# Zero products in the state's PSUM bank, a strided read of the turned r, and new order tables, in an RWKV and MLP-mixer kernel

## The chip, the cores and the metric

The kernel runs on one core of one Trainium2 chip. A core has five engines with a queue each: TensorE (PE; its weight loads are shown as PEld), VectorE (DVE), ScalarE (ACT), GpSimd (POOL) and SyncE (SP), which here only starts transfers. 16 DMA engines move data between the chip's memory, the on-chip memory SBUF and, for transposes, within SBUF. TensorE writes to PSUM, eight banks of 512 fp32 columns on 128 partitions. The metric is the device time of one execution in microseconds (us), lower is better.

## The reference

Two steps, all in fp32 for the reference. First a linear attention with decay over 768 steps, for 4 batches and 8 heads of 48 columns; then a mixer on its result, `x`, with 768 tokens of 384 columns:

```python
for t in range(S):
    cur = np.einsum('bhd,bhe->bhde', u[None] * kt, vt)
    y[:, :, t] = np.einsum('bhd,bhde->bhe', rt, state + cur)
    state = w[None, :, :, None] * state + np.einsum('bhd,bhe->bhde', kt, vt)
...
h = np.maximum(xt @ w_tok1, 0.0) @ w_tok2
u = x + h.transpose(0, 2, 1)
h2 = np.maximum(u @ w_ch1, 0.0) @ w_ch2
return (u + h2).astype(np.float32)
```

`w_tok1` is 768 by 256, `w_tok2` 256 by 768, `w_ch1` 384 by 1536, `w_ch2` 1536 by 384; `xt` is `x` with tokens and columns exchanged.

## The kernel before

**Tiles.** The steps of a batch are cut into six units of 128, so there are 24 units. Heads lie in pairs, four pairs of two heads, each head padded from 48 to 64 columns. In a unit (`unit`, line 539) k is multiplied by powers of the decay (`kr<-kt,wn`), and r by the inverse powers, so that a unit's scores are plain products of k and r. Both are turned, so that head columns lie on partitions; `scores` (line 649) makes the products of turned k and turned r (`at_ps`, eight of 128 columns); two masked copies (`AT`) follow on DVE; `outputs` multiplies them with v (`vb`, v as bf16) and adds the state times r (`y_ps`); each step's own term is v times a sum over r, u and k (`adg`, then `yd` or `ydb`). The result goes to `x_b`. The state is collected in a PSUM tile `kv_ps` (`add_state`, line 666), over three units at a time, and copied to SBUF after each unit (`keep_state`, line 679).

**Batch 0 and the others.** In batch 0 r comes in windows of two units (`window`, line 513): `rwin` holds even and odd steps side by side, two products with powers (`wp2`) fill the two halves of `krw`, eight PE transposes make `tr_ps`, whose layout is (partition, odd or even, pair, step), and `evac_r` (line 530) brings even and odd steps together in `rkb`. k is turned by four transposes (`trk`) and copied to `rka`. Its own terms come from a product of turned k and r (`pr`) and four small matmuls (`ad_ps`), and are added by PE (`ydb` through the identity). Batch 1 turns k and r together on PE (`tr_ps`, `rk`); batches 2 and 3 turn them by DMA. `krw` and `kr` tiles have padding columns, set to zero once at the start (lines 371 to 373).

**Mixer** (`mixer`, line 744). Per batch: `h1_ps` (12 products of 384 columns, from `x_b` and `wtok1`), `h1r` (ReLU), then for batches 0 and 1 `hx_ps`, which gathers turned `x` and the product with `wtok2`, and `uT`, its copy; for batches 2 and 3 `hT_ps`, `u_sb` and a DMA transpose to `uT`. Then, for two halves of the batch, twelve `z_ps` (three products of 384 each, `wch1` times `uT`), their ReLU `zr`, and for each of three units twelve products `h_ps` (`zr` times `wch2`), `osb` and a store. The first `z_ps` of batch 0 is the first of 288.

**Order.** Nothing is scheduled while the program is built: every piece of work is recorded as a task (`Plan`, line 189), and `run` issues the tasks in the order of the table `ORDER` (line 21). Each engine executes its own part of that order strictly. `BUFS` (line 66) says which buffer of a pool each tile takes, `ENGINES` (line 159) which of two engines runs a task that may run on either (`flex`). `W_DEP` and `GATES` (lines 170, 171) tie weight transfers to loads and loads to weight transfers: a transfer with such an entry is not started before the named one has landed. Loads and stores are started by SP, in that order, too, weight transfers by POOL. A transfer is also not started before the one eight places earlier in the round of semaphores has landed.

All engine calls go through one helper, so that nearly every row of the profile has line 263; rows are told apart by their tiles. The profile leaves numbers at the end of names out: `h1_ps` and `h2_ps` are both `h_ps` there, `wtok1` and `wtok2` are `wtok`, `wch1` and `wch2` `wch`, `wp2` `wp`; `h1r`, `kr0` and `krw0` appear as `h1r`, `kr` and `krw`.

**Zero products.** `keep_warm` (line 926) multiplies a tile of zeros by a tile of zeros; nothing reads its result. `NWARM` (line 172) of them, 11, stand in `ORDER`, with 512 columns each and a PSUM buffer of the pool `m`, as other tasks have. The pool `m` has seven buffers, the state's `kv` one, eight banks together.

**The start.** ACT starts four small loads of w and u (`w_row`, `u_row`, `w_heads`, `u_heads`; lines 340 to 345), loads its function table (line 346), and computes powers of w as exponentials: `lnw`, then `wn`, `wp2` and `wp`, each 384 columns.

Of the kernel before, what the change touches and what calls it, by code (L numbers as in the profile page):

```python
# [67 lines left out]
    0, 1, 2, 0, 1, 2, 0, 1, 2, 0, 2, 0, 1, 2, 0, 1, 2, 1, 0, 1, 2, 0, 1, 0,  # L68
],
    'AT1': [  # L70
    0, 1, 2, 0, 1, 2, 0, 1, 2, 0, 2, 0, 1, 2, 0, 1, 0, 1, 2, 1, 0, 2, 1, 0,
# [11 lines left out]
    0, 1, 2, 3, 4, 0, 1, 2, 3, 0, 4, 1, 3, 4, 0, 2, 1, 3, 0, 4, 1, 3, 2, 0,  # L83
# [5 lines left out]
    0, 1, 2, 3, 1, 0, 3, 2, 1, 0, 3, 0, 0, 3, 2, 1, 0, 2, 3, 0, 2, 1, 2, 0,  # L89
# [5 lines left out]
    0, 1, 2, 3, 4, 5, 0, 2, 3, 1, 4, 5, 0, 2, 3, 1, 4, 0, 5, 2, 3, 1, 4, 0,  # L95
],
    'ku': [
    0, 1, 2, 0, 1, 0, 1, 2, 1, 0, 1, 2, 1, 0, 2, 2, 2, 2,
# [13 lines left out]
],  # L112
    'osb': [
    0, 1, 2, 2, 0, 2, 0, 2, 1, 2, 2, 0, 1, 0, 2, 1, 0, 2, 1, 0, 2, 1, 0, 2, 1,
# [5 lines left out]
    0, 1, 2, 3, 0, 2, 3, 1, 0, 2, 3, 0, 2, 1, 0, 3, 1, 0,  # L120
],
    'rka': [
    0, 1, 2, 1, 1, 0,
# [5 lines left out]
    0, 1, 0, 1, 0, 1, 0, 1, 0, 1, 0, 1, 0, 1, 0, 1, 0, 1,  # L129
],  # L130
    'rt': [
    0, 1, 2, 3, 4, 0, 2, 3, 1, 4, 0, 3, 4, 0, 3, 1, 4, 0,
],
    'rwin': [
    0, 1, 2,
],
    'uT': [
    0, 1, 2, 3, 0, 1, 3, 2,
],
    'u_sb': [  # L140
    0, 1, 2, 1,
],
    'vb': [
    0, 1, 2, 3, 4, 0, 1, 2, 3, 4, 0, 1, 2, 2, 4, 3, 0, 2, 0, 4, 1, 2, 4, 0,
],
    'vt': [
    0, 1, 2, 3, 4, 5, 0, 1, 2, 3, 4, 5, 0, 1, 2, 3, 4, 5, 0, 1, 2, 4, 3, 5,
],
    'yd': [
    0, 1, 2, 0, 1, 0, 1, 2, 0, 1, 0, 2, 1, 0, 2, 0, 1, 1,  # L150
],
    'ydb': [
    0, 1, 0, 1, 0, 1,
],
    'zr': [
    0, 1, 2, 0, 1, 0, 2, 0,
],
}
ENGINES = [
# [64 lines left out]
def kernel(  # L224
# [70 lines left out]
    def row(src):  # L295
        return src.rearrange("h d -> (h d)")
# [68 lines left out]
    def make_mask():  # L365
        pool.memset(mask, 1.0)
        pool.affine_select(out=mask, in_=mask, compare_op=ALU.is_gt, fill=0.0, base=0, pattern=[[1, 128]],
                           channel_multiplier=-1)

    t_mask = once("POOL", "mask", make_mask)  # L370
    t_kw0 = [once("DVE", "memset_m", lambda t=t: dve.memset(t, 0.0)) for t in krws]
    t_kp0 = [once("DVE", "memset_m", lambda t=t: dve.memset(t[:, 0], 0.0)) for t in krs]
    t_rp0 = [once("DVE", "memset_m", lambda t=t: dve.memset(t[:, 1], 0.0)) for t in krs]

# [588 lines left out]
```

## Time and profile before

| | us |
|---|---|
| median of 3 runs (169.28 to 170.26) | 170.03 |
| the profiled execution, its own time | 169.46 |
| its span, first to last instruction | 167.6 |
| PE busy (1449 matmuls) | 157.2 |
| DVE busy | 132.1 |
| POOL busy | 72.7 |
| ACT busy | 72.4 |

| group of rows | count | mean ns |
|---|---|---|
| PE `z_ps`, 384 columns | 288 | 327 |
| PE `h_ps` from `wch` and `zr`, 384 columns | 276 | 326 |
| DVE `AT` from `at_ps` and mask | 48 | 681 |
| DVE `rkb` from `tr_ps`, 1024 elements | 2 | 1280 |
| ACT `rkb` from `tr_ps`, 1024 elements | 1 | 1303 |
| DVE `rk` from `tr_ps`, 1024 elements | 2 | 692 |
| ACT `rk` from `tr_ps`, 1024 elements | 4 | 1013 |
| PE `idle_ps`, zero products of 512 columns | 11 | 537 |

The span is what the profiler saw, from the first to the last instruction; the execution's own time has some 1.9 us around it. A PE row's mean is the time one matmul takes from start to end; matmuls overlap, so the distance from one to the next is shorter (51 `z_ps` products follow each other in 8.29 us, 163 ns each), and the distance is what a sum needs. PEclk is the clock that TensorE was granted as a share of full speed. A DMA share is how busy the 16 DMA engines are on average; overlapping packets can bring it over 1.

### The profile page before, as it was taken

To read this page: it belongs to the slowest core of one execution; us is meant where nothing else is said; L and a number is where in the kernel's file an instruction comes from. 1 tells how busy PE (TensorE), PEld (TensorE's weight loads), DVE (VectorE), ACT (ScalarE), POOL (GpSimd) and SP (SyncE) were. 2 spreads that over 40 slices of the span, in tenths; PEclk is the share of its full clock that TensorE was granted. 3 is DMA by queue.
4 is the path that set the end of the run, shared out by engine and by line. 5 is a ranking of instruction groups with operands and counts; after the bars stand their busy time and mean duration, and the time that the engine had idled before them with its cause. 6 is when DMAs were issued, how large, how long until landed. Compare 5 with 4: busy or idle time off the path is not lost.

```text
span 167.6 us, 3756 instructions
## 1 busy us (share of the span) xinstructions
PE 157.2 (94%) x1449; PEld 105.9 (63%) x1449; DVE 132.1 (79%) x257; ACT 72.4 (43%) x158; POOL 72.7 (43%) x88
## 2 busy tenths in 40 slices
PE   6696999799999999999999999999999999999991
PEld 2273768566766777776656666667666666666671
DVE  7899978985898699999699999988988248446322
ACT  3991856467540475577934224156401201504100
POOL 4043956676344737459796789962100000000000
PEclk9999557999999999999999999999999999999999
DMA  5999998999999369899999999999510143501122
GB/s 112 243 250 193 214 183 162 176 188 209 221 209 215 75 152 234 190 201 203 160 209 219 227 204 213 158 254 234 125 47 0 51 101 111 117 0 53 47 94 94
DMA packets 94997, 26.59 MB, mean 159 GB/s; under 512 B 89730, under 2 KB 94084, under 8 KB 94980
## 3 DMA queue, kind: packets, MB, share of 16 engines
q1 hardware_dynamic: 92624, 23.11, 67.9%
q0 software_dynamic: 2160, 3.15, 11.5%
q8 instruction: 11, 0.18, 0.5%
q10 hardware_dynamic: 196, 0.11, 0.2%
q14 instruction: 6, 0.05, 0.1%
HBM read 20.46 MB, written 4.72 MB: 150 GB/s over the span
## 4 chain that ended last, share of the span: by engine, by line
PE 62%; DMA 13%; POOL 7%; DVE 7%; SPq 3%; issue 2%; ACT 2%; ACTq 1%; POOLq 0%
PE h_ps L263 24%; PE z_ps L263 21%; DMA rt<-in_r_dram 5%; PE y_ps L263 4%; PE at_ps L263 4%; SPq L263 3%; POOL rku L263 3%; DMA uT<-u_sb 3%; DMA kt<-in_k_dram 3%; PE tr_ps L263 2%; POOL kr L263 2%; DMA wp<-in_w_dram 2%; PE kv_ps L263 2%; DVE krw L263 2%; DVE rkb L263 1%
## 5 line engine op out<-in xcount | busy, mean ns | idle before, releaser
L263 PE MATMUL h_ps<-wch,zr 128*128 128x384 bf16 (+1 forms) x300 | 53.6, 320 | 0.0
L263 PE MATMUL z_ps<-uT,wch 128*128 128x384 bf16 x288 | 52.0, 327 | 0.7 <-DMA uT<-u_sb 0.4
L263 ACT ACTIVATE zr<-z_ps 128x384 bf16<-128x384 f32 x59 | 28.5, 491 | 35.2 <-PE z_ps L263 30.2
L263 PEld LDWEIGHTS <-wch 128*128 128x128 bf16 x288 | 31.6, 114 | 14.3 <-DMA uT<-u_sb 0.5
L263 PEld LDWEIGHTS <-zr 128*128 128x128 bf16 x300 | 27.4, 98 | 15.5
L263 DVE TENSOR_TENSOR AT<-at_ps,mask 128x512 bf16<-128x512 f32 x48 | 31.0, 681 | 1.6 <-PE at_ps L263 1.4
L263 DVE TENSOR_SCALAR zr<-z_ps 128x384 bf16<-128x384 f32 x37 | 19.8, 554 | 11.4 <-PE z_ps L263 11.3
L263 POOL TENSOR_TENSOR yd<-vb,adg 128x384 f32<-128x384 bf16 x13 | 11.9, 919 | 14.1 <-DVE adg L263 7.1
L263 POOL TENSOR_TENSOR kr<-kt,wn 128x384 bf16<-128x384 f32 x12 | 12.8, 1068 | 5.1 <-PE tr_ps L263 3.3
L263 PEld LDWEIGHTS <-kr 128*128 128x128 bf16 x152 | 11.3, 107 | 5.5 <-issue 3.8
L263 POOL TENSOR_TENSOR rku<-ku,rt 128x384 f32<-128x384 f32 x12 | 12.2, 1026 | 5.8 <-DMA rt<-in_r_dram 3.2
L263 ACT CAST vb<-vt 128x384 bf16<-128x384 f32 x18 | 9.2, 513 | 12.3 <-DMA vt<-in_v_dram 8.4
L263 DVE TENSOR_TENSOR osb<-u_sb,h_ps 128x384 f32<-128x384 bf16 (+1 forms) x13 | 6.8, 523 | 9.3 <-PE h_ps L263 9.1
L263 POOL TENSOR_TENSOR kr<-rt,wp 128x384 bf16<-128x384 f32 x10 | 10.3, 1033 | 5.0 <-DMA rt<-in_r_dram 4.9
L263 PEld LDWEIGHTS <-rk 48*128 48x128 bf16 (+1 forms) x204 | 7.9, 95 | 5.0 <-issue 2.8
L263 POOL TENSOR_TENSOR ku<-kt,u_bc 128x384 f32<-128x384 f32 x10 | 10.4, 1042 | 1.2 <-DMA kt<-in_k_dram 1.1
L263 ACT CAST S<-kv_ps 48x192 bf16<-48x192 f32 x26 | 8.1, 313 | 5.7 <-PE kv_ps L263 5.4
L263 DVE TENSOR_TENSOR x_b<-y_ps,yd 128x384 bf16<-128x384 f32 x18 | 9.8, 552 | 0.8 <-PE y_ps L263 0.7
L263 DVE TENSOR_REDUCE adg<-rku 128x8 f32<-128x384 f32 x18 | 9.7, 545 | 0.5 <-POOL rku L263 0.4
L263 DVE TENSOR_TENSOR kr<-kt,wn 128x384 bf16<-128x384 f32 x12 | 8.4, 703 | 1.7 <-DMA kt<-in_k_dram 1.7
L263 PE MATMUL y_ps<-vb,AT 128*128 128x48 bf16 x192 | 9.2, 188 | 0.0
L263 PEld LDWEIGHTS <-wtok 128*128 128x128 bf16 x72 | 6.8, 98 | 3.8
(96 smaller groups left out, 205.8 us busy)
## 6 DMA issues: line engine op xcount, KB each, us to landing
kt<-in_k_dram SPq DMA_DIRECT2D x24, 192.0 KB, 4.3
vt<-in_v_dram SPq DMA_DIRECT2D x24, 192.0 KB, 3.9
out_dram<-osb SPq DMA_DIRECT2D x23, 192.0 KB, 2.4
rt<-in_r_dram SPq DMA_DIRECT2D x18, 192.0 KB, 4.4
wch<-in_moe_w_ch_dram POOLq DMA_DIRECT2D x4, 384.0 KB, 6.6
rwin<-in_r_dram SPq DMA_DIRECT2D x3, 384.0 KB, 4.4
wtok<-in_moe_w_tok_dram POOLq DMA_DIRECT2D x2, 384.0 KB, 6.0
wch<-in_moe_w_ch_dram POOLq DMA_DIRECT2D x1, 768.0 KB, 9.6
```

The costliest lines, as they stand in the source:

```text
L263: return lambda *args, **kw: tc.keep_in_program_order(f(*args, **kw))
```

## The change

1. `NWARM` goes from 11 to 153. A zero product has 128 columns instead of 512 and takes no buffer of pool `m`: the state's tile is now a whole bank of 512 columns, of which the state has the first 384, and zero products write the last 128. The very first ones, before there is a state, take a bank of their own of the same buffer. All of them are placed in the first batch, up to the first `z_ps`.
2. `evac_r` copies the same elements in another order: it now reads `tr_ps` alternating between even and odd steps (1024 bytes apart) and writes `rkb` in one run; before, it read in runs and wrote every other element.
3. The zeroing of `kr` and `krw` can run on DVE or POOL, and `krw` is zeroed in halves. The function table's load stands behind the load of `w_row`.
4. `ORDER`, `BUFS`, `ENGINES`, `W_DEP` and `GATES` are new: other orders on all engines, other engines for a part of the tasks, one entry in `GATES` in place of four, and the zero products' places.

```diff
-W_DEP = [(0, 4, 1), (0, 3, 0), (1, 0, 0), (1, 0, 1), (1, 1, 2), (1, 1, 0), (1, 1, 1)]
-GATES = {(1, 5, 1): 5, (1, 5, 2): 1, (3, 0, 1): 4, (3, 3, 0): 1}
-NWARM = 11
+W_DEP = [(0, 1, 2), (0, 4, 2), (0, 3, 2), (0, 5, 2), (1, 0, 0), (1, 1, 1), (1, 4, 0)]
+GATES = {(1, 2, 2): 1}
+NWARM = 153
...
-    t_tab = once("ACT", "act_table", lambda: act.preload_act_table_set("natural_log_exp_and_others"))
+    t_tab = once("ACT", "act_table", lambda: act.preload_act_table_set("natural_log_exp_and_others"), [t_wrow])
...
-    t_kw0 = [once("DVE", "memset_m", lambda t=t: dve.memset(t, 0.0)) for t in krws]
-    t_kp0 = [once("DVE", "memset_m", lambda t=t: dve.memset(t[:, 0], 0.0)) for t in krs]
-    t_rp0 = [once("DVE", "memset_m", lambda t=t: dve.memset(t[:, 1], 0.0)) for t in krs]
-
+    ZERO = {"DVE": "memset_m", "POOL": "memset_mp"}
+
+    def zero(t):
+        return flex(ZERO, lambda on: engine_of[on].memset(t, 0.0))
+
+    t_kp0 = [zero(t[:, 0]) for t in krs]
+    t_rp0 = [zero(t[:, 1]) for t in krs]
+
+    t_kw0 = [zero(t[:, j]) for t in krws for j in range(2)]
...
-    kv = [None]
+    kv, bank = [None], [None]
+
+    def new_bank(tag):
+        bank[0] = psum.tile([128, 512], f32, name="kv_ps", tag=tag, bufs=1)
+
...
-            copy(on, W["ra"].rearrange("p a c t -> p a (c t)").rearrange("p a (s j) -> p j a s", j=2), W["tr"])
+            copy(on, W["ra"].rearrange("p a c t -> p a (c t)").rearrange("p a (s j) -> p a s j", j=2),
+                 W["tr"].rearrange("p j a s -> p a s j"))
...
-                kv[0] = ps("kv_ps", [128, HP, 2, D], of="kv")
+                new_bank(f"kv{plan.buf('kv')}")
+                kv[0] = bank[0][:, 0:dm].rearrange("p (a q d) -> p a q d", a=HP, q=2)
...
     def keep_warm():
-        z = ps("idle_ps", [128, 512])
-        pe.matmul(z, warm[:, 0:128], warm, start=True, stop=True)
+        fresh = bank[0] is None
+        if fresh:
+            new_bank("kv0")
+        pe.matmul(bank[0][:, dm:512], warm[:, 0:128], warm[:, 0:128], start=fresh, stop=True, skip_group_check=True)
 
     for _ in range(NWARM):
-        add("PE", "warm", keep_warm, [t_warm], take=("m",))
+        add("PE", "warm", keep_warm, [t_warm])
```

The kind names in quotes (`"memset_mp"`, `"copy1024w"`) only label tasks and reach no engine. What the tables do to the work around the first batch, as the built order has it: 37 zero products come before the first `at_ps` product, 116 between it and the first `z_ps`. Of the products that scale k and r in batch 0, six run on POOL in place of two, one after the other: half of r window 0, `kr2`, `kr3`, half of r window 1, `kr3` again, half of r window 2. On DVE no work of batch 1 stands ahead of batch 0's `h1r`; before, two products of k or r, one of k and u, and one cast of v did. Eight transposes, eight scores and four state products of batch 1 stood ahead of the first `z_ps` on PE and now follow it. ACT's load of `w_heads` waits for the first load of k to land.

More of the change, by code (lines that the diff above doesn't have):

```diff
@@ L67 @@
     'AT0': [
-    0, 1, 2, 0, 1, 2, 0, 1, 2, 0, 2, 0, 1, 2, 0, 1, 2, 1, 0, 1, 2, 0, 1, 0,
+    0, 1, 2, 0, 1, 2, 1, 2, 0, 2, 0, 1, 2, 0, 1, 2, 0, 1, 2, 1, 0, 2, 0, 1,
 ],
     'AT1': [
-    0, 1, 2, 0, 1, 2, 0, 1, 2, 0, 2, 0, 1, 2, 0, 1, 0, 1, 2, 1, 0, 2, 1, 0,
+    0, 1, 2, 0, 1, 2, 0, 2, 1, 2, 1, 0, 2, 1, 0, 2, 1, 0, 2, 0, 1, 2, 1, 0,
 ],
@@ L82 @@
     'adg': [
-    0, 1, 2, 3, 4, 0, 1, 2, 3, 0, 4, 1, 3, 4, 0, 2, 1, 3, 0, 4, 1, 3, 2, 0,
+    0, 1, 2, 3, 4, 1, 2, 0, 3, 1, 4, 0, 3, 2, 1, 4, 0, 3, 2, 1, 0, 3, 4, 2,
 ],
@@ L88 @@
     'kp': [
-    0, 1, 2, 3, 1, 0, 3, 2, 1, 0, 3, 0, 0, 3, 2, 1, 0, 2, 3, 0, 2, 1, 2, 0,
+    0, 1, 2, 3, 3, 0, 2, 1, 3, 0, 3, 3, 1, 2, 3, 0, 1, 1, 2, 1, 0, 3, 1, 3,
 ],
@@ L94 @@
     'kt': [
-    0, 1, 2, 3, 4, 5, 0, 2, 3, 1, 4, 5, 0, 2, 3, 1, 4, 0, 5, 2, 3, 1, 4, 0,
+    0, 1, 2, 3, 4, 5, 0, 1, 2, 3, 4, 5, 0, 1, 2, 4, 3, 5, 0, 1, 2, 4, 3, 0,
 ],
     'ku': [
-    0, 1, 2, 0, 1, 0, 1, 2, 1, 0, 1, 2, 1, 0, 2, 2, 2, 2,
+    0, 1, 2, 1, 2, 1, 0, 2, 1, 0, 1, 0, 2, 1, 2, 2, 0, 0,
 ],
@@ L103 @@
     'm': [
[8 rows of a table removed]
[8 rows of a table added]
 ],
     'osb': [
-    0, 1, 2, 2, 0, 2, 0, 2, 1, 2, 2, 0, 1, 0, 2, 1, 0, 2, 1, 0, 2, 1, 0, 2, 1,
+    0, 1, 2, 0, 0, 2, 2, 1, 2, 0, 1, 0, 2, 0, 1, 2, 0, 1, 2, 0, 1, 2, 0, 1, 2,
 ],
@@ L119 @@
     'rk': [
-    0, 1, 2, 3, 0, 2, 3, 1, 0, 2, 3, 0, 2, 1, 0, 3, 1, 0,
+    0, 1, 2, 3, 1, 3, 0, 2, 1, 3, 0, 1, 3, 2, 1, 0, 2, 3,
 ],
     'rka': [
-    0, 1, 2, 1, 1, 0,
+    0, 1, 2, 2, 0, 1,
 ],
@@ L128 @@
     'rku': [
-    0, 1, 0, 1, 0, 1, 0, 1, 0, 1, 0, 1, 0, 1, 0, 1, 0, 1,
+    0, 1, 0, 1, 0, 1, 0, 1, 0, 1, 1, 0, 1, 0, 1, 0, 0, 1,
 ],
     'rt': [
-    0, 1, 2, 3, 4, 0, 2, 3, 1, 4, 0, 3, 4, 0, 3, 1, 4, 0,
+    0, 1, 2, 3, 4, 1, 0, 2, 4, 3, 0, 1, 4, 3, 1, 0, 4, 2,
 ],
@@ L137 @@
     'uT': [
-    0, 1, 2, 3, 0, 1, 3, 2,
+    0, 1, 2, 3, 1, 0, 3, 2,
 ],
     'u_sb': [
-    0, 1, 2, 1,
+    0, 1, 2, 0,
 ],
     'vb': [
-    0, 1, 2, 3, 4, 0, 1, 2, 3, 4, 0, 1, 2, 2, 4, 3, 0, 2, 0, 4, 1, 2, 4, 0,
+    0, 1, 2, 3, 4, 0, 1, 2, 3, 4, 0, 2, 1, 4, 3, 1, 2, 0, 2, 1, 4, 1, 0, 2,
 ],
     'vt': [
-    0, 1, 2, 3, 4, 5, 0, 1, 2, 3, 4, 5, 0, 1, 2, 3, 4, 5, 0, 1, 2, 4, 3, 5,
+    0, 1, 2, 3, 4, 5, 0, 1, 2, 3, 4, 5, 0, 1, 2, 3, 4, 5, 0, 1, 2, 3, 4, 5,
 ],
     'yd': [
-    0, 1, 2, 0, 1, 0, 1, 2, 0, 1, 0, 2, 1, 0, 2, 0, 1, 1,
+    0, 1, 2, 0, 1, 2, 1, 0, 2, 1, 1, 2, 0, 2, 1, 1, 0, 2,
 ],
     'ydb': [
-    0, 1, 0, 1, 0, 1,
+    0, 1, 0, 0, 1, 0,
 ],
     'zr': [
-    0, 1, 2, 0, 1, 0, 2, 0,
+    0, 1, 2, 0, 1, 0, 2, 1,
 ],
@@ L340 @@
     t_wrow = once("ACT", "dma_tiny", lambda: act.dma_start(w_row, row(w).unsqueeze(0)))
-    t_wh = once("ACT", "dma_tiny", lambda: act.dma_start(
+    t_wh = once("ACT", "dma_tiny2", lambda: act.dma_start(
         w_heads.rearrange("h (q d) -> h q d", q=2)[:, :, 0:D], w.unsqueeze(1).to_broadcast([H, 2, D])), [t_wh1])
-    t_urows = once("ACT", "dma_tiny", lambda: act.dma_start(
+    t_urows = once("ACT", "dma_tiny2", lambda: act.dma_start(
         u_heads.rearrange("h (q d) -> h q d", q=2)[:, :, 0:D], u.unsqueeze(1).to_broadcast([H, 2, D])), [t_uh0])
-    t_urow = once("ACT", "dma_tiny", lambda: act.dma_start(u_row, row(u).unsqueeze(0)))
-    t_tab = once("ACT", "act_table", lambda: act.preload_act_table_set("natural_log_exp_and_others"))
+    t_urow = once("ACT", "dma_tiny2", lambda: act.dma_start(u_row, row(u).unsqueeze(0)))
+    t_tab = once("ACT", "act_table", lambda: act.preload_act_table_set("natural_log_exp_and_others"), [t_wrow])
     t_ones = once("DVE", "memset_s", lambda: dve.memset(ones, 1.0))
@@ L536, in window @@
         t_tr = add("PE", "tr_all", turn_r, [m0, m1, t_id], take=("m",), use=[(m0, "krw")])
-        W["t"] = flex({"ACT": "copy1024", "DVE": "copy1024d"}, evac_r, [t_tr], take=("rkb",), use=[(t_tr, "m")])
+        W["t"] = flex({"ACT": "copy1024w", "DVE": "copy1024v"}, evac_r, [t_tr], take=("rkb",), use=[(t_tr, "m")])
     def unit(b, c):
```

129 rows, old and new, of tables (BUFS, ENGINES, ORDER) are left out of this document.

## The prediction

> **What bounds the kernel now.** I read the page's slices first, then the busy time of TensorE (PE) in stretches, then the chain of waits, then the instructions in order of time. The slices of the profiled execution (40 equal parts of 167.6 us, 4.19 us each):
>
> ```profile
> PE   6696999799999999999999999999999999999991
> DVE  7899978985898699999699999988988248446322
> POOL 4043956676344737459796789962100000000000
> PEclk9999557999999999999999999999999999999999
> DMA  5999998999999369899999999999510143501122
> ```
>
> From slice 9 on PE is full almost to the end, so time can be saved only before that, in the first batch. There slices 5 to 7 show a granted clock of half speed. The stretches between the points where the clock changes are 3.41 us long; columns are stretch, its length, PE busy (instructions), clock, DMA share, GB/s:
>
> ```profile
> 10.22:13.63 3.41, 3.13 (x22) 1.00 1.09 211
> 13.63:17.04 3.41, 2.11 (x26) 1.00 1.06 207
> 17.04:20.45 3.41, 3.04 (x50) 0.50 1.10 219
> 20.45:23.87 3.42, 3.12 (x41) 0.50 1.13 177
> 23.87:27.28 3.41, 3.41 (x48) 0.50 1.00 172
> 30.69:34.10 3.41, 2.22 (x28) 1.00 1.05 153
> ```
>
> After the stretch with 2.11 us busy the clock fell; the one with 2.22 us did not lose it. It came back after 3.13 and after 3.41 us, not after 3.04 or 3.12. So here the clock is held by about 2.2 us of work in 3.41, and won by about 3.13. The 1.00 before 13.63 us is no measurement: the chain has four transposes of 128 columns in 0.43 us there, and eight in 0.45 us later, so TensorE ran at half speed (107 ns a product) up to about 13.6 us and again from 17.0 to 27.3, and at full speed (56 ns) otherwise.
>
> ```profile
> 8.29 0.43 PE trk L263 x4
> ...
> 29.40 0.63 DVE kr L263
> 30.03 1.27 DVE ku L263
> 31.30 1.10 DVE vb L263
> 32.40 0.47 DVE kr L263
> ...
> 36.81 8.29 PE z_ps L263 x51
> ...
> 47.92 0.45 PE tr_ps L263 x8
> ```
>
> The chain also shows VectorE (DVE) spending 3.47 us on products and a cast of the second batch just before the first batch's last `h1r`. From the first `z` at 36.81 us PE runs on to 164.25 with 0.7 us of waits; the last store ends at 167.6. I call the first scores product that waits for `rkb` S (16.30 us), the first `z` Z (36.81 us); Z to the end is 130.8 us.
>
> **The change, part by part.** Counts are from the built order of the changed kernel, durations from rows of before.
>
> *Zero products.* 11 of 512 columns go, 153 of 128 columns come: 37 before S, 116 between S and Z, none later. At 56 ns the 116 cost 6.5 us of PE's queue, at 107 ns 12.4 us. They are in order, so each holds back what is behind it unless PE would have waited.
>
> *S.* Four of the first batch's early products (half of r windows 0 and 1, `kr2`, `kr3`) go from DVE to GpSimd (POOL): six POOL products in a row (0.96 us apart, rows of 1.00) from about 6.6 us, when the second power for r is done. DVE loses 1.2 us of memsets ahead of `kr0`, which then starts when its power is ready, near 5.1 instead of 5.99 us. POOL's six memsets of 512 columns are unseen: its row for 128 columns is 0.20 us, so 0.2 to 0.8 each; I take 0.5, 3 us in all, done by 5.9 and hidden ahead of the first product at 6.6 (at 0.8 they would add 1 us). ScalarE's `w_heads` load now waits for the first k load, and `lnw` stands behind it; k loads land 2.8 to 5.7 us after their issue, this one's is at 0.81, so 3.6 to 6.5, against `lnw` at 3.91; I take the early end, 0.1 us, since nothing is loading yet. On PE the first window's transposes stand behind `ud`, and that behind `kr1`, `rka` and a small product on DVE: about 9.6 us. Then, at half speed, eight transposes (0.87), `trk` (0.43), 15 zero products (1.61), `trk` (0.43; its k load is SP's sixth, lands near 10.4, and POOL takes 1.0) and 6 zero products (0.64): S = 13.6 us, 2.7 sooner; 12 if the clock is up, 15.6 if DVE is held up (below).
>
> *The turned r.* Three evictions read with a step and write in one run. Rows: 1.28 us (DVE) and 1.30 (ScalarE) with the stepped write; 0.69 and 1.01 for 1024 elements with no step. No row has a stepped read: from 0.69 to twice the stepped row, 2.6. I take 1.28, no change, the row that still has a step: the first then ends before 13 us and PE arrives later; the others lie beside PE's work. At 2.6 S would be 14.4 and the time 169.4. The Trainium skill ("SBUF — State Buffer", section "Door 1: The DMA port swizzle") speaks against this edit: lines of 16 bytes in SBUF and 8 in PSUM, and a penalty for each access that goes to a new line. The old write steps by 4 bytes and stays in a line four times; the new read steps by 1024 bytes and changes lines at each element, so by it the new eviction is the dearer one and 169.4 the sum. That the old step should then have cost nothing does not agree with 1.28 against 0.69 us.
>
> *S to Z.* PE's real work at full speed: 48 scores at 41 ns (2.0), outputs 48 at 25 and 20 at 42 ns (2.0), states 24 at 42 ns and one 384 (1.2), six `ydb` at 163 (1.0), 24 transposes and 18 `hx` at 56 (2.4), 24 `ad` at 25 (0.6), 24 of `h1` and `hx` at 163 (3.9): 13.1 us. With 6.5 us of zero products 19.6. DVE's list from `rkb` to `h1r` (twelve masks at 0.60, five `pr` at 0.33, seven others at 0.47, small ones) is 13.2 us, and from `h1r` to Z another 2.9: below PE's, since the 3.47 us of second-batch work are gone. So PE becomes the bound of this stage. Half speed after S: with PE fed, one stretch should win the clock; half a stretch on average is 1.7 us at half speed, 0.85 us lost (0 to 5.1). Three zero products wait for ScalarE's copy of the state from the same bank, with scores, `ad` and outputs behind them; the copy (0.65 a pair) ends near PE's arrival: 0.4 us (0 to 1.5). Z = 13.6 + 13.1 + 6.5 + 0.85 + 0.4 = 34.45, 2.36 us sooner.
>
> *After Z.* Of the second batch, 8 transposes, 8 scores and 4 state products, done ahead of Z before, now follow: 0.45 + 0.33 + 0.17 = 0.95 us. `wch1_1` (9.6 us to land) is triggered behind a POOL product that needs `ad`, and from that `ad` to the first use PE has 9.3 us of work: 0 to 1.5, I take 0, as other waits of PE will lie between. Loads must follow a Z that is 2.4 us sooner. They are full (share 1.05 to 1.16) from 4 to 118 us but for one hole, where a store waits at the head of SP's queue:
>
> ```profile
> 54.00:60.00 6.00, 6.00 (x81) 4.36 (x79) 4.00 (x8) 3.18 (x5) 3.82 (x4) 1.00 0.37 72
> 60.00:98.00 38.00, 37.70 (x419) 25.94 (x417) 36.32 (x68) 21.30 (x48) 25.48 (x26) 1.00 1.09 204
> ```
>
> A share of 0.37 over 6 us leaves 3.8 us; with Z sooner that store is ready sooner, so up to 3.8 us can be followed. The new load order and gates I price at -0.3 to 2 us, at 0. Products move from DVE (9.6 us less, of 132.1) to POOL (12 more, on 72.7): both stay below PE's 157.
>
> Sum: -2.36 + 0.95 = -1.4 us. Against the profiled execution: span 167.6 to 166.2, its time 169.46 to 168.1. That execution lay 0.6 us below the median of 170.03, so the median becomes 168.6.
>
> **Rivals.**
> *The clock stays down (slower).* The zero products sit in PE's queue; at 107 ns they cost 12.4 us. If PE runs 10.2 us at half speed after S, as it did before, Z = 13.6 + 19.6 + 5.1 + 0.4 = 38.7, +1.9, with 0.95 more: +2.85, 172.9 us. It decides from 4.5 us at half speed after S. For: stretches of 3.04 and 3.12 us busy did not win the clock, and waits for POOL's products leave such holes. Against: at half speed PE has the longest list, so it fills its own stretch.
> *POOL locks DVE out (no change).* Rows at 11.45 us:
>
> ```profile
> 11.45 2.41 DVE L263 TENSOR_TENSOR krw<-rwin,wp 128x384 bf16<-128x384 f32 x1
> 11.48 1.01 POOL L263 TENSOR_TENSOR kr<-kt,wn 128x384 bf16<-128x384 f32 x1
> 12.44 1.00 POOL L263 TENSOR_TENSOR krw<-rwin,wp 128x384 bf16<-128x384 f32 x1
> ```
>
> A DVE product of 0.55 us waited until two POOL products were over. Now six stand in a row from 6.6, at the worst to 12.4; then `kr1` to `rkb` on DVE (3.2 us) make S 15.6, Z 36.45, -0.36 + 0.95 = +0.6: 170.6. Against: POOL itself waits for k loads near 10 us and lets DVE in. The Trainium skill ("SBUF — State Buffer", section "SBUF: two separate sides") calls it an exclusive lock held for a whole instruction; the 2.41 us agree.
> *Loads set the pace (no change).* If the hole stays, the third batch's last `x_b` (97.4 us) comes no sooner, and PE's 66.2 us behind it, alike in both orders, end where they did: 170.0.
> *All of it works (faster).* Clock up before S, S at 12.0, no waits: Z = 31.6, -5.2 + 0.95 = -4.3; loads allow -3.8: 166.2.
>
> **How the numbers follow.** Runs of before lie within 0.6%, so 0.5% (0.85 us) is what counts as a change. Forecast 0.42; all works 0.13; clock down 0.20; lock 0.12; loads 0.13. The forecast's own range is 167 to 170. Faster: nearly all of the forecast and the last rival, 0.53. Same: loads, most of the lock, a little of the forecast, 0.22. Slower: clock and the rest of the lock, 0.25. The range of 165.8 to 173 leaves out the far end of the clock case and less than a tenth below.
>
> **What would show it.** Right: clock 1.00 from near 14 us on, zero products at 56 ns spacing, first masked scores before 15 us, first `z` near 34.5, from it 131.7 us to the end. Wrong: a half clock past 18 us, `z` after 36; DVE products over 2 us between 7 and 12 us; `rkb` evictions far from 1.28 us; PE waits for `uT`, `kt` or `wch` after 40 us of more than 1.5 us in sum; a DMA hole that is as wide as before.

## The result and the profile after

The changed kernel takes 176.74 us (median of 4 runs, 176.16 to 177.47), beside 169.66 us of the kernel before on the same chip (4 runs, 168.47 to 170.26): 1.0429 times as long, 95% interval 1.0349 to 1.0508. The profiled execution's span went from 167.6 to 175.8 us. The forecast was 1.4 us less, and it is 8.2 us more. Ratios, here and below, and the times given with them leave out executions more than 1.5% above the fastest of their kernel, though four profiles below are of such executions: without the 116 (171.16 us), zero products alone (175.67), the lock by itself (174.18) and the moved store beside all zero products (174.99).

The prediction divided the span at two points: S, the first scores product that waits for `rkb`, and Z, the first `z_ps` product. Below, Z is read from the instructions in order of time for every kernel (36.65 for the one before; the chain has 36.81).

| us | S | S to Z | Z | Z to the end | span |
|---|---|---|---|---|---|
| before | 16.30 | 20.35 | 36.65 | 130.95 | 167.6 |
| forecast | 13.6 | 20.85 | 34.45 | 131.75 | 166.2 |
| after | 12.97 | 29.24 | 42.21 | 133.6 | 175.8 |

S came as forecast. S to Z is 8.4 us longer than forecast, Z to the end 1.9 us. The page's slices of the kernel after (40 of 4.40 us):

```profile
PE   5999889099999999999999999869999999999992
DVE  7867778932669898999999985959986328424422
POOL 8568935952019299785999983369500000000000
PEclk9999999759999999999999999999999999999999
DMA  5999999999950059999999989999920053302122
```

The eighth slice (from 30.8 us) has a 0 for PE, with DVE at 9 and POOL at 9; the clock falls to 7 in it and 5 in the next. Slices 26 and 27 (from 109.9 us) have a second, smaller hole in PE. The same first batch in stretches of 3.41 us (columns: stretch, its length, busy PE, PEld, DVE, ACT, POOL, clock, DMA share, GB/s):

```profile
17.04:20.45 3.41, 3.41 (x77) 3.10 (x75) 2.45 (x5) 3.12 (x9) 3.01 (x5) 1.00 1.27 190
20.45:23.87 3.42, 2.26 (x37) 1.57 (x34) 3.02 (x6) 1.34 (x5) 1.60 (x2) 1.00 1.16 184
23.87:27.28 3.41, 3.33 (x53) 2.56 (x53) 2.16 (x6) 1.88 (x5) 1.39 (x2) 1.00 0.93 179
27.28:30.69 3.41, 3.30 (x72) 2.93 (x70) 3.31 (x5) 1.27 (x4) 2.16 (x3) 1.00 1.00 184
30.69:34.10 3.41, 0.00 (x0) 0.00 (x0) 3.41 (x1) 0.00 (x0) 3.41 (x5) 0.88 1.18 219
34.10:37.51 3.41, 2.74 (x13) 1.53 (x13) 1.37 (x3) 0.00 (x0) 2.00 (x3) 0.50 1.17 223
37.51:40.92 3.41, 3.41 (x28) 2.74 (x27) 0.83 (x2) 1.12 (x3) 1.67 (x2) 0.62 1.10 214
```

Up to 30.7 us the clock is up, as the forecast had it (eight scores take 0.40 us at 12.97 and at 26.76). In the stretch from 30.69 PE does nothing and DVE executes one instruction for the whole stretch. The instructions in order of time (start, duration, engine, operation, tiles; in brackets the idle time before and what ended it) say which:

```profile
29.65 5.06 DVE L272 TENSOR_TENSOR ydb<-vb,adg 128x384 bf16<-128x384 bf16 x1
...
30.11 1.01 POOL L272 TENSOR_TENSOR kr<-kt,wn 128x384 bf16<-128x384 f32 x1
...
31.07 1.00 POOL L272 TENSOR_TENSOR ku<-kt,u_bc 128x384 f32<-128x384 f32 x1
...
32.02 0.99 POOL L272 TENSOR_TENSOR kr<-rt,wp 128x384 bf16<-128x384 f32 x1
32.97 0.99 POOL L272 TENSOR_TENSOR rku<-ku,rt 128x384 f32<-128x384 f32 x1
...
34.77 0.48 PE L272 MATMUL y_ps<-ydb,ident 128*128 128x384 bf16 x1 [4.17 <-DVE ydb L272]
```

In the kernel before:

```profile
28.38 0.55 DVE L263 TENSOR_TENSOR ydb<-vb,adg 128x384 bf16<-128x384 bf16 x1
```

The first batch's last `ydb` on DVE, a product of 0.55 us in the kernel before, takes 5.06 us. It ends once POOL's row of four products of the second batch is over. PE waits for it for 4.17 us, and restarts at half speed: clock 0.88, 0.50 and 0.62 in the three stretches.

Behind Z, the longest wait of PE is for a v of the last batch. From the instructions in order of time, SP's queue and that wait:

```profile
106.18 3.31 SPq L272 DMA_TRANSPOSE rk<-kr  x2
...
109.58 0.53 SPq L272 DMA_DIRECT2D out_dram<-osb  x1
...
110.16 0.43 SPq L272 DMA_DIRECT2D vt<-in_v_dram  x1
...
115.23 0.51 ACT L272 CAST vb<-vt 128x384 bf16<-128x384 f32 x1 [3.96 <-DMA vt<-in_v_dram]
...
115.79 0.33 PE L272 MATMUL kv_ps<-vb,kr 128*128 128x96 bf16 x4 [2.16 <-ACT vb L272]
```

That load stands in the new order behind two DMA transposes and a store; it is issued at 110.16 and used at 115.23. In the kernel before PE waits no longer than 0.37 us for anything behind Z. The hole in the DMA row, which the forecast hoped would narrow, is wider: slices 13 and 14 (52.7 to 61.5 us) show 0, while SP waits for the first store.

The evictions of the turned r, from the groups of instructions (count, busy us, mean ns):

```profile
L272 ACT COPY rkb<-tr_ps 128x1024 bf16<-128x1024 bf16 x2 | 2.0, 1018 | 0.0
...
L272 DVE COPY rkb<-tr_ps 128x1024 bf16<-128x1024 bf16 x1 | 1.2, 1224 | 0.2 <-PE tr_ps L272 0.2
```

On ACT 1.02 us (1.30 before), on DVE 1.22 (1.28 before).

### The profile page after: what moved, and what is told of

Same layout as the page of the kernel before. It is cut to its first block, busy times and chain, and to the rows that moved or that the text cites. A ratio compares the mean times of both kernels' runs of the same rounds, so it can differ in the third digit from the quotient of the medians.

```text
span 175.8 us, 4042 instructions
## 1 busy us (share of the span) xinstructions
PE 162.7 (93%) x1591; PEld 113.4 (65%) x1591; DVE 125.6 (71%) x237; ACT 73.9 (42%) x165; POOL 85.6 (49%) x103
## 3 DMA queue, kind: packets, MB, share of 16 engines
HBM read 20.46 MB, written 4.72 MB: 143 GB/s over the span
## 4 chain that ended last, share of the span: by engine, by line
PE 67%; POOL 13%; issue 6%; DVE 5%; DMA 4%; ACT 1%; SPq 1%; POOLq 1%; DVEq 0%; ACTq 0%
PE h_ps L272 25%; PE z_ps L272 17%; PE kv_ps L272 8%; POOL kr L272 6%; PE hx_ps L272 4%; PE y_ps L272 3%; DVE ydb L272 3%; POOL ku L272 3%; PE at_ps L272 3%; POOL rku L272 2%; PE tr_ps L272 2%; DMA rk<-kr 2%; POOL yd L272 2%; DMA kt<-in_k_dram 2%; PE trk L272 1%
## 5 line engine op out<-in xcount | busy, mean ns | idle before, releaser
L272 PE MATMUL z_ps<-uT,wch 128*128 128x384 bf16 x288 | 52.7, 327 | 0.0
L272 PEld LDWEIGHTS <-zr 128*128 128x128 bf16 x300 | 27.4, 98 | 15.6
L272 DVE TENSOR_SCALAR zr<-z_ps 128x384 bf16<-128x384 f32 x35 | 18.5, 552 | 12.1 <-PE z_ps L272 12.1
L272 POOL TENSOR_TENSOR kr<-kt,wn 128x384 bf16<-128x384 f32 x19 | 20.5, 1077 | 5.7 <-DMA kt<-in_k_dram 3.1
L272 POOL TENSOR_TENSOR ku<-kt,u_bc 128x384 f32<-128x384 f32 x15 | 16.3, 1091 | 8.3 <-DVE rku L272 5.3
L272 PE MATMUL kv_ps<-warm 128*128 128x128 bf16 x153 | 16.8, 249 | 3.2 <-DVE warm L272 1.8
L272 POOL TENSOR_TENSOR kr<-rt,wp 128x384 bf16<-128x384 f32 x12 | 12.4, 1044 | 8.6 <-PE tr_ps L272 8.4
L272 PEld LDWEIGHTS <-warm 128*128 128x128 bf16 x153 | 12.0, 113 | 6.3 <-issue 3.5
L272 POOL TENSOR_TENSOR yd<-vb,adg 128x384 f32<-128x384 bf16 x11 | 9.8, 892 | 8.1 <-ACT vb L272 4.3
L272 POOL TENSOR_TENSOR rku<-ku,rt 128x384 f32<-128x384 f32 x10 | 10.8, 1079 | 0.2
L272 ACT ACTIVATE h1r<-h_ps 128x384 bf16<-128x384 f32 x6 | 2.7, 489 | 19.2 <-PE h_ps L272 19.2
```

The source lines that it names most:

```text
L272: return lambda *args, **kw: tc.keep_in_program_order(f(*args, **kw))
```

## The experiments

Ratios are to the kernel before, run beside each on the same chip, with 95% intervals. The task tables are changed by entries, counted from 0.

**The last `ydb` on POOL.** The wait on DVE is taken away by moving the one product.

```diff
 ENGINES, entry 65 (own part, batch 0, unit 5)
-1
+0
```

> The changed kernel, but the last ydb product of the first batch (own part of unit 5) runs on POOL, ahead of POOL's row of four products, in place of DVE, where it took 5.06 us. Theory A (DVE is locked out while POOL runs products in a row, and the clock falls in the hole this makes on PE): ydb ends near 30.9 us, PE's hole of 4.17 us goes, the clock stays at 1.00, first z near 35.5 us in place of 42.3, the later wait for v of 2.2 us mostly goes too, as loads follow; time 168.5 to 170.5. Theory B (the 116 zero products fill PE's queue, and the lock only takes time that they would take): first z near 39 us, time 173 to 175. Theory C (the time is lost behind the first z, in the new load order): first z moves, the end does not, time 174 to 177.

Measured: 173.39 us (172.5 to 175.01), ratio 1.0308 (1.0194 to 1.0423). Z is at 35.95 and the clock 1.00 in all stretches up to it, as theory A says; PE's hole is gone. From the instructions in order of time:

```profile
14.74 0.22 PE L276 MATMUL kv_ps<-warm 128*128 128x128 bf16 x1 [0.21 <-ACT S L276]
...
21.47 0.33 PE L276 MATMUL kv_ps<-warm 128*128 128x128 bf16 x3 [0.72 <-DVE S L276]
...
24.02 0.22 PE L276 MATMUL kv_ps<-warm 128*128 128x128 bf16 x1 [0.47 <-ACT S L276]
...
31.08 0.32 PE L276 MATMUL y_ps<-ydb,ident 128*128 128x384 bf16 x1 [0.41 <-POOL ydb L276]
```

The span is 170.8, 5.0 us less; the ratio's interval overlaps that of the changed kernel (1.0349 to 1.0508). But the time misses theory A's range by 3 us: Z to the end is 134.9, and PE waits 1.90 us for the same v. So the lock is real, and it is not the whole loss. The three other waits are zero products that wait for the state's copy out of the bank they share with it, 1.4 us together.

**No zero products behind S.** Zero products behind the first scores are left out of `ORDER`, 116 of 153, with the lock and without it.

```diff
-NWARM = 153
+NWARM = 37
```

> The changed kernel without the 116 zero products that stand behind the first scores; 37 stay. Theory A: DVE's last ydb product still stands beside POOL's row of products, so PE still waits for it, first z 40 to 43 us and time 174 to 177, with the clock at half speed for a part of the stage before as well. Theory B: PE's queue loses 6.5 us of work; first z 4 us or more sooner, time 170 to 172.5.

> Both edits: the last ydb on POOL, and no zero product behind the first scores. If the zero products hold the clock and lie in PE's gaps (forecast), this is slower than the kernel with the last ydb on POOL alone, by 0.5 to 3 us, with a granted clock of 0.5 in some stretches between 14 and 34 us. If they are in the way (theory B), it is faster by 1 to 4 us with the clock as good, or lower.

Measured without the 116: 167.88 us (six executions, 167.4 to 168.49), ratio 0.9944 (0.9908 to 0.998), below the ranges of both theories. In the profiled execution, which took 171.16 us, DVE is locked as before; whether it is in the six faster ones, no trace shows:

```profile
26.40 4.72 DVE L261 TENSOR_TENSOR ydb<-vb,adg 128x384 bf16<-128x384 bf16 x1
```

Z is at 36.88 there and the span 169.4. With the last `ydb` on POOL as well: 166.67 us (three executions), ratio 0.9867 (0.9783 to 0.9951), Z at 31.09, span 163.9. So the ratio falls without the 116 zero products by 0.0485 with the lock and by 0.0441 without it (8.2 and 7.5 us of 169.66); the profiled spans fall by 6.4 and 6.9 us. My expectation that the clock would fall without them failed. The stretches of this last kernel:

```profile
17.04:20.45 3.41, 2.85 (x54) 2.21 (x54) 3.38 (x7) 2.90 (x9) 3.39 (x5) 1.00 1.31 201
20.45:23.87 3.42, 3.03 (x50) 2.19 (x49) 3.21 (x7) 2.56 (x7) 1.90 (x3) 1.00 1.25 218
23.87:27.28 3.41, 2.25 (x36) 1.63 (x34) 1.60 (x4) 0.57 (x2) 3.21 (x4) 1.00 1.13 214
```

PE's own work keeps the clock, with 2.25 us busy in 3.41 too.

**The turned r alone, in the kernel before.**

```diff
-            copy(on, W["ra"].rearrange("p a c t -> p a (c t)").rearrange("p a (s j) -> p j a s", j=2), W["tr"])
+            copy(on, W["ra"].rearrange("p a c t -> p a (c t)").rearrange("p a (s j) -> p a s j", j=2),
+                 W["tr"].rearrange("p j a s -> p a s j"))
```

> The kernel before with one part of the change alone: evac_r reads strided and writes rkb in one run. By the rows of the changed kernel the eviction takes 1.22 us on DVE (1.28 before) and 1.02 on ACT (1.30 before); time within 0.3 us of the kernel before. If the strided read costs more beside other work, rkb over 1.4 us and the time 0.3 us or more up.

Measured: 169.59 us (10 runs), ratio 1.0031 (0.9997 to 1.0065); `rkb` 1.21 us on DVE (1.28 before) and 1.01 on ACT (1.30). The instruction is a little cheaper, the time shows no gain.

**Zero products alone, in the kernel before.**

```diff
+    def zero_product():
+        pe.matmul(bank[0][:, dm:512], warm[:, 0:128], warm[:, 0:128], start=False, stop=True, skip_group_check=True)
+
+    for _ in range(116):
+        add("PE", "zero", zero_product, [t_warm])
```

> The kernel before with one part of the change alone: 116 zero products of 128 columns into the free columns of the state's bank, two or three behind each of PE's pieces of work between the first state product and the first z; its eleven others stay. At 56 ns they cost 6.5 us of PE's queue, at half speed 12.4. If they are paid for in full where PE is the busiest engine of the stage: first z 3 to 6 us later than 36.8, time 172 to 176, with the clock back earlier than 27.3 us. If they lie in gaps and win the clock: first z sooner, time 167 to 169.

The state's tile is a whole bank in this kernel, as in the change. Measured: 173.34 us (two executions, 174.62 and 172.06), ratio 1.022 (1.0091 to 1.035). From the instructions in order of time, the first `z_ps` (in an execution of 175.67 us):

```profile
43.87 2.44 PE L263 MATMUL z_ps<-uT,wch 128*128 128x384 bf16 x14
```

S is 16.46, so S to Z is 27.4 in place of 20.35 us: 7.0 us for 116 products, although the clock is at 1.00 again in the stretch from 23.87 us (from 27.28 before). No other part of the change is in this kernel, and it is slower, by 1.5 to 5.9 us if one goes by the ratio's interval; so the 7.0 us of the one profile are more than the time shows.

**Half of them.** Every second of the 116 is left out, with the last `ydb` on POOL.

```diff
-NWARM = 153
+NWARM = 95
```

> The changed kernel with the last ydb on POOL and every second of the 116 zero products behind the first scores left out (58 stay, and the 37 early ones). With all 116: first z 35.95, 173.4 us; with none: 31.09, 166.9 us. Theory E (each is paid for in PE's queue): first z 33 to 34.2, time 169 to 171. If only the last few in the queue cost, or the clock decides: near one of the ends, within 1 us.

Measured: 169.28 us (seven executions), ratio 0.998 (0.9931 to 1.0029). Z is at 35.04, later than expected, because S is at 14.15 in this execution. S to Z is what the products stand in: 18.72 us with none, 20.89 with 58, 22.91 with 116. That is 2.2 and 2.0 us for each half, a line, with one execution behind each point (a second one with none has 18.72 again). The times are not on a line: the ratio goes from 0.9867 (0.9933 in a second set of runs, below) over 0.998 to 1.0308.

**No zero product at all,** the 37 ahead of S left out too (last `ydb` on POOL).

```diff
-NWARM = 153
+NWARM = 0
```

> The changed kernel with the last ydb of the first batch on POOL and no zero product at all, early ones left out too. If the 37 early ones win the clock: half speed in some stretches between 13 and 28 us, first z 2 to 5 us later than with them (31.09), time 168 to 171. If they do nothing that the kernel's own work does not do: within 0.8 us of 166.9.

Measured: 167.28 us, ratio 0.9862 (0.9794 to 0.9931), no different from 0.9867 with the 37. PE is then at half speed for some 10 us longer. From the instructions in order of time:

```profile
20.13 0.61 PE L263 MATMUL at_ps<-rkb,rka 48*128 48x128 bf16 x8
...
23.71 0.40 PE L263 MATMUL at_ps<-rkb,rka 48*128 48x128 bf16 x8
```

The same eight products take 0.61 and then 0.40 us: the clock came back by 23.7 us (by 12.4 and 12.8 in the two executions with the 37, where the first eight scores take 0.40 us). S to Z is 20.97, 2.25 more than with them, but S is 11.48, 0.9 to 1.3 sooner than in the two executions with them, probably since the 37 hold PE's queue too. Z is 32.45 (31.09 and 31.50). What is left, a microsecond of Z, the time doesn't show.

**The lock by itself.** The last `ydb` stays on DVE and all zero products stay; POOL's row of four goes to DVE, behind the first batch's work.

```diff
 ENGINES, entries 123, 124, 125, 128 (ku, rku, kr of batch 1, unit 2; kr of unit 3)
-0, 0, 0, 0
+1, 1, 1, 1
```

> The changed kernel, the last ydb of the first batch on DVE as in it, all zero products as in it; only POOL's row of four products of the second batch (two kr, ku, rku, 30.1 to 34.0 us) goes to DVE, where it stands behind the first batch's last x_b and h1r. Theory A (lock): with POOL quiet the same ydb takes 0.4 to 0.8 us in place of 5.06, PE's hole of 4.17 us goes, first z 35 to 37 us in place of 42.3, time 171.5 to 174.5. If that ydb is slow for a reason of its own (a wait inside it for its sources): it still takes over 3 us and the time stays at 176.

Measured: 171.33 us (two executions, 170.66 and 172.0), ratio 1.0106 (1.0028 to 1.0184). In the profile Z is at 37.01 and S at 14.23, so S to Z is 22.8, as with `ydb` on POOL (22.9). The product, on the same engine with the same operands, from the instructions in order of time:

```profile
31.35 0.56 DVE L276 TENSOR_TENSOR ydb<-vb,adg 128x384 bf16<-128x384 bf16 x1
```

0.56 us in place of 5.06: what it waited for was POOL's row.

**Behind Z: the first store.** In the new order of SP's queue the first store stands behind 36 load windows, before it was 40, and SP waits for it (11.3 us in the kernel after, 50.7 to 62.1). It is moved four loads back.

```diff
 ORDER (315 is the first store; 85, 86, 105, 82 loads)
-... 315, ... 85, ... 86, ... 105, ... 82, ...
+... 85, ... 86, ... 105, ... 82, 315, ...
```

> The kernel with the last ydb of the first batch on POOL and no zero products behind the first scores, and the first store four loads later in SP's queue (behind 40 load windows, as in the kernel before; the changed kernel has 36). Theory D (behind the first z the time is lost because SP's queue waits with the first store at its head, and the loads behind it come late): SP's wait of 2.9 us before the first store goes, the wait of 0.9 us for v near 104 us goes, from first z to the end 131.5 to 132.3 us in place of 132.8; time 0.3 to 1.2 us less. If the loads wait for buffers anyway: no change.

> The changed kernel with the last ydb of the first batch on POOL and the first store four loads later in SP's queue; the zero products stay. Theory D: of the 7.8 us that SP waits before the first store about 3.8 us go (four loads of 192 KB at some 200 GB/s), so loads that PE waits for later (1.9 us for v near 111 us) come sooner; from first z to the end 132.5 to 133.5 us in place of 134.9, time 171 to 172.5. Otherwise 173.4 as without the move.

Measured without the 116: 167.78 us (three executions), ratio 0.986 (0.9767 to 0.9953), beside 0.9867 without the move; SP's wait of 3.0 us before the store is gone, but Z to the end is 132.8 in both and the wait for v is 0.90 us in both. So theory D's repair gained nothing here. With the zero products: 171.81 us (three executions), ratio 1.012 (1.0028 to 1.0212), beside 1.0308 (1.0194 to 1.0423); the two overlap. In the profile PE's wait for v is 1.86 us (1.90 without the move), Z to the end is 135.3, and the clock fell at 23.9 us:

```profile
20.45:23.87 3.42, 2.64 (x47) 1.97 (x44) 3.13 (x6) 1.36 (x4) 1.84 (x3) 1.00 1.21 211
23.87:27.28 3.41, 2.95 (x40) 2.53 (x35) 1.79 (x5) 1.43 (x4) 1.39 (x2) 0.60 1.08 207
```

So the pair is inconclusive on the store. It does show that the 116 don't always hold the clock: it fell after 2.64 us busy of 3.42, more than the 2.2 us that the forecast took as enough.

**Behind Z: the late v.** That load is moved ahead of the two transposes and the store; the kernel without the move runs beside it.

```diff
 ORDER (111 is r, 106 v of the last batch)
-... 111, ... 106, ...
+... 111, 106, ...
```

> The kernel with the last ydb on POOL and no zero products behind the first scores again, for comparison in the same call: ratio to the kernel before 0.98 to 0.993, time 166 to 168.5.

> The same kernel with one load moved: v of the last batch's first unit stands ahead of two DMA transposes and a store in SP's queue, not behind them (it was issued at 99.7 us, 3.7 us behind the transposes' start, and PE waited 0.9 us for it at 104; in the changed kernel 2.16 us at 113.6). Theory F (the new order of SP's queue makes that load late, and the wait is passed on to the end): the wait goes, from first z to the end 131.9 in place of 132.8, 0.5 to 0.9 us less than no_zero_again. If another wait takes its place: no change.

Measured: 168.15 us (11 executions), ratio 0.9933 (0.9894 to 0.9972), without the move; 168.48 us (12), ratio 0.9935 (0.9899 to 0.997), with it. The wait for v, 1.15 us in the one profile, is not in the other. In its place, in the order of time:

```profile
104.80 0.40 PE L265 MATMUL at_ps<-rk 48*128 48x128 bf16 x8 [1.91 <-DMA rk<-kr]
```

A transposed k and r that now comes behind the load is late instead. Theory F has the wait right and the remedy wrong: in both orders something in that part of SP's queue is late. Z to the end is 134.6 in both; it was 132.8 in the first profile of the kernel without the move, so it varies by 1.8 us between executions of one kernel.

## Why the prediction was wrong

The spans add up, with the points that the forecast used: 166.2, less 0.6 (S sooner than forecast), plus 2.1 (S to Z without the lock, 22.9 for 20.85), plus 6.3 (the lock, 29.2 for 22.9), plus 1.9 (Z to the end), is 175.8 after rounding.

**S** was right: 12.97 for 13.6, with the first window's transposes at 9.01 for "about 9.6" and the rest in the forecast order; the clock was up by 12.97. S lies between 12.37 and 14.23 us in the executions with the same work ahead of it, so the 0.6 us say little.

**The turned r** was right: no change, 1.22 and 1.02 us for the 1.28 taken. The Trainium skill ("SBUF — State Buffer", section "Door 1: The DMA port swizzle") gives SBUF lines of 16 bytes with a penalty for each access that crosses to a new line, and PSUM lines of 8 bytes. Taken for PSUM too, it makes the new read, which changes PSUM lines at each element, the dearer form. Here it is not: 1.02 us against 1.30 with the stepped write, on the same engine.

**The zero products** were mis-sized against what they buy. The forecast put 6.5 us on PE's path; in this order they cost 4.2 (22.91 less 18.72), because PE would have waited for a part of that, and in the order of the kernel before 7.0 by its one profile. Their wait for the state's copy, put at 0.4, is 1.4 us and lies in the 4.2. Together the two terms came out smaller than forecast. Whether zero products in a bank of their own would cost less was not run. The error is in the rest of the stage: "PE's real work at full speed ... 13.1 us", with 0.85 and 0.4 for clock and waits 14.35. The stage takes 18.72 without any zero product behind S, with clock 1.00: PE is busy for 15.4 us of it and idle for 3.3, in short waits for masks, `adg`, states, `kr` and `ydb` (the longest 0.93, for `ydb` on POOL). The step that failed is "So PE becomes the bound of this stage": the sum of PE's work, from the spacing of products in a run, is not the length of the stage. That results going back and forth between four engines make the difference is the reading of those waits; no run takes one of them away. And the clock did not need the 116 in the traced executions without them: they were added where the clock was already won, or was won soon after S. Nor is half speed as dear as the rival of the clock reckoned (5.1 us for 10.2 at half speed): with no zero product at all some 10 us more of it made the stage 2.25 us longer.

**The lock** is the step that failed most against the forecast, as it was put at nothing in this place. The forecast counted DVE's list from `rkb` to Z as "below PE's, since the 3.47 us of second-batch work are gone". That work was not gone: a part went to POOL, and there it runs just when DVE's last product of the first batch is due. The rival "POOL locks DVE out" was the right mechanism at the wrong place: I looked for it at S, where six POOL products stand one behind the other, and priced 2 us; there POOL waits in between for a load and for `trk`, and DVE's products took 0.55 to 0.68 us. It decided some 17 us behind S, with a row of four, 5.06 us for 0.55, and cost 6.3 us between S and Z (5.0 without the 116, 23.67 less 18.72): 4.17 in PE's hole, and, it seems, most of the rest at half speed behind it. In the ratios it is 0.0121 (2.1 us, `ydb` on POOL, with overlapping intervals) and 0.0323 (5.5 us, the row on DVE, clear of each other); without the 116 it is not clear of noise (0.9944 beside 0.9867 and 0.9933). The rival of the clock that stays down did not happen as told, but the clock did fall, as a consequence of this hole. The Trainium skill ("SBUF — State Buffer", section "SBUF: two separate sides") describes the lock, for a DVE instruction with two SBUF sources, as held for an instruction. The trace agrees on the kind of instruction; the wait was for four of POOL's, not one. The forecast's own rows had shown two already (2.41 us, through two POOL products).

**Behind Z** the forecast had 0.95 us of moved work, and priced the new load order at 0 of a range of -0.3 to 2. It is 1.9 us more than that, at the end of the range; the wait for v alone is 2.16 us. That the late loads come from the new order of SP's queue is the likely reading, but not shown: two moves of single entries took no time away, the part that PE waits for changes with them, and two profiles of one kernel differ by 1.8 us here. Z to the end is 132.5 to 135.5 us in all kernels that have the new order, 129.9 to 131.4 in those with the old one.

So of the parts, the zero products behind S cost most (7.5 to 8.2 us by the ratios), the lock next (2.1 to 5.5 beside them), and the rest of the change together is a gain of about one per cent: without both, 0.9867 (0.9783 to 0.9951) of the kernel before in one set of runs and 0.9933 (0.9894 to 0.9972) in another. What in the rest makes the gain was not taken apart.

## What to carry to other kernels

Filler work for the clock is worth only what wins the clock; once it is won, see whether the kernel's own work keeps it (here it did with 2.25 us busy in 3.41, while it was lost once after 2.64, so the busy time alone doesn't tell), since further products in an in-order queue are paid for in good part (116 products, 6.5 us of PE's queue, made the stage 4.2 us longer). When work moves from DVE to POOL, list what POOL executes in a row beside each DVE product with two SBUF sources over the whole stage, not only where the move was made. The longest sum of one engine is a lower bound of a stage, not its length, where results go back and forth between engines.

## What the runs showed that I had not expected

A DVE product with both sources in SBUF did not get in between POOL's instructions, though its row begins 0.46 us ahead of the first of them: it ended 0.75 us after the last of four (and took 4.72 us beside the same four without the zero products). Why it did not run at its start, the traces don't show. A DVE instruction that reads PSUM was not held back: `x_b` took 0.56 us at 35.29 beside POOL's `kr` of 34.53 to 35.57.

The clock column can read 1.00 while PE is at half speed: in the kernel with no zero product at all these two stretches have 1.00,

```profile
17.04:20.45 3.41, 3.41 (x50) 2.44 (x46) 2.93 (x5) 2.42 (x7) 3.36 (x5) 1.00 1.26 177
20.45:23.87 3.42, 3.42 (x40) 2.21 (x38) 2.69 (x7) 2.32 (x6) 1.79 (x3) 1.00 1.23 214
```

and the eight scores products at 20.13 us in the first take 0.61 us, those at 23.71 in the second 0.40. The durations of equal groups tell the speed here; the column did not.
